# The last keys of V by halves of the heads in a fused decode kernel

## The chip, the cores and the metric

The kernel runs on one core of a Trainium2 chip. The metric is the device time of one execution in microseconds; the time before is the median of three runs.

## The reference

Two branches work on the same eight tokens and are mixed by a gate:

```python
q = (x @ wq).reshape(B, Sq, H, Dh).transpose(0, 2, 1, 3)         # B 8, Sq 1, D 576, H 32, Dh 128
scores = einsum("bhqd,bhkd->bhqk", q, k_cache) * (Dh ** -0.5)    # Sk 4096 keys
o = einsum("bhqk,bhkd->bhqd", softmax(scores), v_cache)
a = o.transpose(0, 2, 1, 3).reshape(B, Sq, H * Dh) @ wo
b = gelu(layernorm(x) @ w1 + b1) @ w2 + b2                       # hidden 4608
g = sigmoid((x * gate_w).sum(-1))
return g * a + (1 - g) * b
```

All tensors are bf16. The K and V caches, 268 MB each, are nearly all the bytes.

## The kernel before

The attention is cut into 32 groups. A group is one token and eight heads (`HB`). Its K (or V) is 8 MB and lies on 128 partitions: sixteen partitions (`RH`) for each head, 256 keys on each partition. Partitions 0 to 63 so hold heads 0 to 3 of the group, and 64 to 127 heads 4 to 7.

For each group VectorE multiplies K with the query in eight chunks (`mult`, line 465), TensorE sums the products (lines 476 and 179), VectorE reduces them (line 484) and runs the softmax, and TensorE multiplies the probabilities with V (`pv`, line 527). In `pv` the probabilities are the stationary operand, and a tile `P` holds them spread over the eight heads with zeros where partition and head don't match (`own`). ScalarE evicts the sums (`evict`), TensorE gathers them by head (`gather`, line 545), and VectorE normalises.

Instructions are recorded in order for each engine by `op`, and semaphore waits are worked out from the records that an operation names. All bulk loads are issued by SyncE, in the order in which they are recorded; a load waits until its buffer is free. `load` gives a transfer a semaphore of its own.

The last group (`last`) is handled apart. Its V arrives in eight pieces (`V_LAST`, keys per partition), into the buffer `VL`, a view of K's. The first 192 keys of each partition go through `pv`. For the rest, from `T_TURN` on, the roles are turned (`pv_turned`, line 653): V is the stationary operand, one matmul for each key of a partition, and the sums for eight heads appear as columns 0 to 7 of the PSUM bank `qb_ps`; `gather` adds the first 192 keys there. `norm_turned` (line 662) multiplies by the reciprocal sums `rz` and writes into `OT_sb`, and `a_proj` runs the last eight heads through the output projection, four matmuls for each head (`quarters`, line 590). The projections of the other 24 heads are done before. Last, line 735 combines both branches, and four stores write the output.

The bias `b2` is broadcast from memory into rows of `b2_4`, in four groups that begin at partitions 0, 32, 64 and 96, of which eight rows each are used in the output. `load_b2` issues its transfers on ScalarE's queue, at the fourth group before the last; `b_gate` on GpSimd adds it.

Of the kernel before, what the change touches and what calls it, by code (L numbers as in the profile page):

```python
# [6 lines left out]
ACT = mybir.ActivationFunctionType  # L7
ALU = mybir.AluOpType
AX = mybir.AxisListType
BF16 = mybir.dt.bfloat16  # L10
F32 = mybir.dt.float32
# [11 lines left out]
HB = 8  # L23
RH = 128 // HB
NHG = H // HB
NG = NHG * B
NTT = SK // RH
# [7 lines left out]
TQ = 4  # L35
QN = D // 4
# [5 lines left out]
class Stream:  # L42
# [10 lines left out]
    def op(self, engine, fn, waits=(), dma=None, side=0):  # L53

        rec = [fn, [w for w in waits if w is not None], None, dma, (engine, side)]
        self.ops[engine].append(rec)
        if dma is not None:
            return ("dma", *dma)
        return ("op", engine, rec)
# [81 lines left out]
def bass_gated_mix__mha_block_cached__mixer_channel_mlp__decode_kernel(  # L141
# [18 lines left out]
    op = S.op  # L160
# [4 lines left out]
    def pstride(t):  # L165
        return t[tuple([slice(None)] * len(t.shape))].ap[0][0]

    def view(t, offset, shape):
        ap = []
        stride = 1  # L170
        for n in reversed(shape[1:]):
            ap.insert(0, [stride, n])
            stride *= n
        return bass.AP(tensor=t, offset=offset, ap=[[pstride(t), shape[0]]] + ap)
# [23 lines left out]
    VL = view(KR, 0, [128, NTT, DH])  # L198
    p1 = sb("p1", [128, 2, CT, DH], BF16)

    P_last = view(p1, 0, [128, NTQ, HB, TQ])
# [19 lines left out]
    b2_4 = sb("b2_4", [128, QN], BF16)  # L221
# [5 lines left out]
    q_bc = sb("q_bc", [128, B, NHG * DH], BF16)  # L227
    OT_sb = sb("OT_sb", [128, H, B], BF16)
    bmg_sb = view(up_f, 0, [128, QN])
    out_sb = sb("out_sb", [128, QN], BF16)  # L230
    g4 = sb("g4", [128, 2], F32)
    ident = sb("ident", [128, 128], BF16)
# [6 lines left out]
    shift = sb("shift", [128, SW + 128], BF16)  # L239
# [4 lines left out]
    mB = sb("mB", [128, 32], F32)  # L244
# [10 lines left out]
    rz = sb("rz", [128, HB], F32)  # L255
# [4 lines left out]
    o_ps = bank[2:4]  # L260
    qb_ps = bank[4]
    oz_ps = bank[5]
    up_ps = bank[6]
# [7 lines left out]
    def load(engine, dst, src, name, waits=()):  # L271
        return op(engine, lambda e: e.dma_start(dst, src), waits, dma=(nc.alloc_semaphore(name), 16))  # L272
# [8 lines left out]
    c_b2 = op("gpsimd", lambda e: e.memset(b2_4[:], 0.0))  # L281
# [12 lines left out]
    def kv_src(cache, n):  # L294
        hg, b = divmod(n, B)
        return cache[b, hg * HB:(hg + 1) * HB].rearrange("h (p t) d -> (h p) t d", p=RH)

    k_done, v_done = {}, {}
    k_land, v_land = {}, {}
# [24 lines left out]
        t = op("sync", lambda e: e.dma_start(dst, src), [*waits, v_done.get(n - 1)], dma=(sV, 16 * nV[0]))  # L324
        v_land[n] = [(t, VB, 0, 0, NTT)]

    def load_v_part(n, buf, at, t0, t1, waits):

        src = kv_src(A_v_cache, n)[:, t0:t1, :]
        dst = buf[:, at:at + t1 - t0, :]  # L330
        t = load("sync", dst, src, f"sVp{n}_{t0}", waits)
        v_land.setdefault(n, []).append((t, buf, at - t0, t0, t1))

    V_LAST = (128, 32, 32, 16, 16, 16, 8, 8)
    T_TURN = NTK + 64

    last = NG - 1
    load_k_half(0, 0)
# [17 lines left out]
    def blank(ps):  # L356
# [5 lines left out]
        out=own[:, :], in_=ident[:, :].rearrange("p (h r) -> p h r", h=HB), axis=AX.X, op=ALU.add), [c_id])  # L362
    c_fine = aside("vector", lambda e: e.tensor_reduce(
        out=fine[:, :], in_=bass.AP(tensor=ident, offset=0, ap=[[pstride(ident), 128], [1, RD], [RD, RH]]),
        axis=AX.X, op=ALU.max), [c_id])
    c_shift = aside("vector", lambda e: e.tensor_reduce(
        out=shift[:, SW:SW + RH], in_=ident[:, :].rearrange("p (a r) -> p a r", r=RD), axis=AX.X, op=ALU.max),
        [c_id, c_shift])
    c_Sel = aside("scalar", lambda e: e.activation(
        out=Sel[:].rearrange("p b (h r) -> p b h r", h=4),  # L370
        in_=bass.AP(tensor=ident, offset=0, ap=[[pstride(ident), 128], [1, B], [32, 4], [0, RH]]), func=ACT.Copy), [c_id])


    t = op("vector", lambda e: e.tensor_reduce(out=stat[:, 0:1], in_=x_sb, axis=AX.X, op=ALU.add), [ld_x])
    t1 = op("vector", lambda e: e.tensor_tensor_reduce(out=junk, in0=x_sb, in1=x_sb, scale=1.0, scalar=0.0,
                                                       op0=ALU.mult, op1=ALU.add, accum_out=stat[:, 1:2]))
    t = op("vector", lambda e: e.tensor_scalar(out=stat[:, 2:3], in0=stat[:, 0:1], scalar1=1.0 / D, scalar2=None,
                                               op0=ALU.mult), [t])
    t = op("vector", lambda e: e.tensor_tensor(out=stat[:, 3:4], in0=stat[:, 2:3], in1=stat[:, 2:3], op=ALU.mult), [t])
    t = op("vector", lambda e: e.scalar_tensor_tensor(out=stat[:, 6:7], in0=stat[:, 1:2], scalar=1.0 / D,  # L380
                                                      in1=stat[:, 3:4], op0=ALU.mult, op1=ALU.subtract), [t, t1])
# [30 lines left out]
    t = op("vector", lambda e: e.reciprocal(out=stat[:, 7:8], in_=stat[:, 5:6]), [a_sqrt])  # L412
# [8 lines left out]
    for half in range(2):  # L421
        for h in range(4):
            for kt in range(NKT):
                o = tr_ps[half][32 * h:32 * h + B, :]
                at = (kt * SK + half * (SK // 2) if kt < NKF else NKF * SK) + h * DH
                r = bass.AP(tensor=VB, offset=at, ap=[[pstride(VB), 128], [4 * DH, 4], [1, DH]])
                xi = kt if kt < NKF else NKF + half
                p_Q = aside("tensor", lambda e, o=o, r=r, kt=kt, xi=xi: e.matmul(
                    o, lhsT=xT_sb[:, xi, :], rhs=r, start=(kt == 0), stop=(kt == NKT - 1)),
                    [v_xT, *ld_wq, *c_ps] if h == kt == half == 0 else ())  # L430
        a_Q.append(aside("scalar", lambda e, half=half: e.activation(
            out=Q4[:, half * 512:(half + 1) * 512], in_=tr_ps[half][:, :], func=ACT.Copy, scale=inv_sqrt_dh), [p_Q]))
# [5 lines left out]
    a_qb, v_mult, v_red, p_sum, v_nm, a_exp, v_P, p_pv, a_ev, p_oz, v_norm, v_rs, p_z, v_rz = ({} for _ in range(14))  # L438
# [9 lines left out]
    a_q, a_O = {}, {}  # L448
# [71 lines left out]
    def pv(n, parts):  # L520
        for i in parts:
            land, buf, shift, t0, t1 = v_land[n][i]
            for tq in range(t0 // TQ, t1 // TQ):
# [5 lines left out]
                    rhs=buf[:, at:at + TQ, :].rearrange("p t d -> p (t d)"),  # L529
                    start=(tq < 4), stop=(tq >= (NTQ if n < last else T_TURN // TQ) - 4)), w)  # L530
        v_done[n] = p_pv[n]
# [6 lines left out]
    def evict(n):  # L538
        a_ev[n] = op("scalar", lambda e: e.activation(out=O_sb[:].rearrange("p t d -> p (t d)"), in_=o_ps[n // last][:, :],  # L539
                                                      func=ACT.Copy), [p_pv[n], p_oz.get(n - 1)])  # L540
# [15 lines left out]
    st = {}  # L556
# [30 lines left out]
    def quarters(lhsT, w, first, stop, waits, end=aside):  # L587

        for i in range(4):
            last = (end if i == 3 else aside)("tensor", lambda e, i=i: e.matmul(  # L590
                y_ps[32 * i:32 * i + B, 0:QN], lhsT=lhsT, rhs=w[:, i * QN:(i + 1) * QN], start=first, stop=stop),
                waits if i == 0 else ())
        return last

    def load_b2():
        st["ld_b2"] = [
            load("scalar", b2_4[32 * i + r:32 * i + r + m, :],
                 bass.AP(tensor=B_b2.tensor, offset=B_b2.offset + i * QN, ap=[[0, m], [1, QN]]), f"ld_b2{i}_{r}", [c_b2])
            for i in range(4) for r, m in ((0, 5), (5, 3))]

    def down_proj(j0, j1):
        for jt in range(j0, j1):
# [36 lines left out]
            out=o.rearrange("p r b -> p (r b)"), in_=up_ps[:, 0:RD * B], func=ACT.Copy), [st["p_rows"]])  # L639
        st["rows", hg] = st["a_rows"]  # L640

    def a_proj(hg):
        for h in range(hg * HB, (hg + 1) * HB):
            st["p_a"] = quarters(OT_sb[:, h, :], wo_sb[:, h, :], h == 0, h == H - 1,
                                 [st.get(("rows", hg)), a_O.get(min(hg * B + B - 1, NG - 2)), v_norm.get(NG - 1),
                                  st["ld_wo" if hg < NHG - 1 else "ld_wo3"], st["a_bx"]] if h == hg * HB else ())


    def pv_turned(n, parts):
        for i in parts:  # L650
            land, buf, shift, t0, t1 = v_land[n][i]
            for t in range(t0, t1):
                p_oz[n] = op("tensor", lambda e, t=t, buf=buf, at=t + shift: e.matmul(  # L653
                    qb_ps[:, 0:HB], lhsT=buf[:, at, :], rhs=P_last[:, t // TQ, :, t % TQ], start=(t == T_TURN), stop=(t == NTT - 1)),
                    [land, v_P[n]] if t == t0 else ())

    def recip(n):
        v_rz[n] = op("vector", lambda e: e.reciprocal(out=rz[:, :], in_=oz_ps[:, HB:2 * HB]), [p_z[n]])

    def norm_turned(n):  # L660
        hg, b = divmod(n, B)
        v_norm[n] = op("vector", lambda e: e.tensor_tensor(  # L662
            out=OT_sb[:, hg * HB:(hg + 1) * HB, b], in0=qb_ps[:, 0:HB], in1=rz[:, :], op=ALU.mult),
            [p_oz[n], v_rz[n]])


    q_of(0)
# [2 lines left out]
    for n in range(NG):  # L670
# [14 lines left out]
        if n == 0:  # L685
# [5 lines left out]
                out=selO[:].rearrange("p t h -> p h t"),  # L691
                in_=bass.AP(tensor=ident, offset=0, ap=[[pstride(ident), 128], [TQ, HB], [1, TQ], [32, 4]]),
# [3 lines left out]
            for i in range(4):  # L696
                a_g4 = aside("scalar", lambda e, i=i: e.activation(out=g4[32 * i:32 * i + B, :], in_=stat[:, G_COL:G_COL + 2],
                                                                func=ACT.Copy), [v_omg, c_g4])
# [19 lines left out]
        if n == last - 4:  # L718
            load_b2()
            b_gate()  # L720
    t0 = 0
    for nt in V_LAST:
        load_v_part(last, VL, t0, t0, t0 + nt, [k_done[last, 0]])
        t0 += nt
    pv(last, (0,))
    total(last)
    recip(last)
    pv(last, (1, 2))
    evict(last)
    pv_turned(last, (3,))  # L730
    gather(last)
    pv_turned(last, range(4, len(V_LAST)))
    norm_turned(last)
    a_proj(NHG - 1)
    t = op("vector", lambda e: e.scalar_tensor_tensor(  # L735
        out=out_sb[0:QP, :], in0=y_ps[0:QP, 0:QN], scalar=g4[0:QP, 0:1], in1=bmg_sb[0:QP, :],
        op0=ALU.mult, op1=ALU.add), [st["p_a"], st["g_bmg"], a_g4])
# [45 lines left out]
```

## Time and profile before

| | |
|---|---|
| median of 3 runs | 1298.17 us (1297.94 to 1298.27) |
| profiled execution | 1298.21 us |
| its span, first to last instruction | 1296.3 us |
| mean granted TensorE clock | 0.834 |
| bytes moved, mean rate over the span | 557.12 MB, 430 GB/s |

The profile is of one execution. PE is TensorE's matmuls, PEld its weight loads, DVE is VectorE, ACT ScalarE, POOL GpSimd, SP SyncE. Times in the trace count from the first instruction of the span; the execution's own time is some 2 us longer than the span. A row of a view names the line of the kernel, the engine, the operation, and `out<-in` by the program's names.

### The profile page before, as it was taken

Reading aid. Unit: us, or ns where it says so; the run is one execution under the profiler, and the core shown is the slowest. Engines: PE = TensorE matmul, PEld = TensorE weight load, DVE = VectorE, ACT = ScalarE, POOL = GpSimd, SP = SyncE. Lnnn points to the kernel's source line nnn. Section 1 sums busy time; section 2 is a strip of 40 time slices with the busy share of each in tenths; the row PEclk is TensorE's granted clock in tenths of the full one; section 3 lists DMA queues with packets and bytes.
Section 4 is the critical chain, followed back from the end, with each engine's and each line's share of the span. In section 5 each row is a group of like instructions: output and inputs, shape, how many; then the busy total and the mean of one; then the engine's idle time right before and its main releaser. Section 6 shows DMA issues by size and latency. Waiting matters only on the chain.

```text
span 1296.3 us, 10765 instructions
## 1 busy us (share of the span) xinstructions
PE 739.2 (57%) x5044; PEld 152.9 (12%) x3252; DVE 851.1 (66%) x1075; ACT 68.8 (5%) x163; POOL 10.4 (1%) x23
## 2 busy tenths in 40 slices
PE   3955556555556555556555556645556655546646
PEld 0521111011111001111001111001111001111003
DVE  3646667766668766667766667766667776667771
ACT  3100000000000000000000000000000000000000
POOL 0010000000000000000000000000000000000000
PEclk8877898778888877888887799878789877888886
DMA  9999999999999999999999999999999999999997
GB/s 405 430 440 429 441 425 433 441 427 441 427 431 441 427 441 429 431 441 427 439 431 431 441 425 439 433 431 441 425 437 435 429 443 425 437 433 431 441 417 327
DMA packets 12987, 557.12 MB, mean 430 GB/s; under 512 B 1568, under 2 KB 2608, under 8 KB 3504
## 3 DMA queue, kind: packets, MB, share of 16 engines
q1 hardware_dynamic: 12704, 556.93, 99.5%
q8 instruction: 7, 0.11, 0.0%
q10 hardware_dynamic: 272, 0.04, 0.0%
q14 instruction: 4, 0.03, 0.0%
HBM read 556.96 MB, written 0.01 MB: 430 GB/s over the span
## 4 chain that ended last, share of the span: by engine, by line
DMA 68%; DVE 19%; PE 9%; issue 3%; SPq 0%; DVEq 0%
DMA KR<-in_A_k_cache_dram 67%; DVE p L465 16%; PE psb L179 7%; DVE s_sb L484 2%; DMA KR<-in_A_v_cache_dram 2%; PE psb L476 2%; SPq L272 0%; DVEq L134 0%; PE psb L590 0%; PE psb L653 0%; DVE out_sb L735 0%; DVE OT_sb L662 0%
## 5 line engine op out<-in xcount | busy, mean ns | idle before, releaser
L465 DVE TENSOR_TENSOR p<-KR,q_n 128x4096 bf16<-128x4096 bf16 x256 | 582.0, 2284 | 229.7 <-DMA KR<-in_A_k_cache_dram 229.7
L179 PE MATMUL psb<-p,ident 128*128 128x512 bf16 x1792 | 482.9, 415 | 0.0
L476 PE MATMUL psb<-p,ident 128*128 128x512 bf16 x256 | 111.4, 435 | 504.5 <-DVE p L465 504.5
L484 DVE TENSOR_REDUCE s_sb<-psb 128x32 f32<-128x512 f32 x256 | 175.2, 684 | 90.8 <-PE psb L179 90.8
L476 PEld LDWEIGHTS psb<-p,ident 128*128 128x128 bf16 x256 | 26.1, 102 | 950.9 <-DVE p L465 950.4
L527 PE MATMUL psb<-VB,P 128*32 128x512 bf16 x1984 | 115.0, 385 | 4.5 <-DMA VB<-in_A_v_cache_dram 4.5
L513 DVE TENSOR_SCALAR P<-E,own 128x256 bf16<-128x256 bf16 x248 | 51.7, 284 | 84.3 <-ACT E L510 84.3
L527 PEld LDWEIGHTS psb<-VB,P 128*32 128x32 bf16 x1984 | 50.6, 98 | 54.4 <-DMA VB<-in_A_v_cache_dram 4.7
L452 ACT ACTIVATE q_n<-q_bc 128x128 bf16<-128x128 bf16 x32 | 9.9, 309 | 865.9 <-DVE p L465 865.9
L545 PE MATMUL psb<-selO,O_sb 128*128 128x8 f32 x256 | 33.9, 259 | 21.8 <-ACT O_sb L539 21.8
L545 PEld LDWEIGHTS psb<-selO,O_sb 128*128 128x128 f32 x256 | 31.0, 191 | 37.1 <-ACT O_sb L539 37.1
L539 ACT ACTIVATE O_sb<-psb 128x512 f32<-128x512 f32 x32 | 19.1, 597 | 176.6 <-PE psb L527 176.6
L566 PE MATMUL psb<-yT_sb,KR 128*128 128x8 bf16 (+1 forms) x216 | 19.6, 229 | 0.0
L566 PEld LDWEIGHTS psb<-yT_sb,KR 128*128 128x128 bf16 (+1 forms) x216 | 18.4, 165 | 2.7 <-issue 1.4
L534 PEld LDWEIGHTS psb<-rs,ones 128*128 128x128 f32 x64 | 12.3, 194 | 46.0 <-issue 45.2
L510 ACT ACTIVATE E<-s_sb,mD 128x256 bf16<-128x256 f32 x32 | 16.0, 499 | 9.7 <-DVE mD L509 9.6
L501 DVE TENSOR_REDUCE mA<-s_sb 128x1 f32<-128x256 f32 x32 | 13.4, 420 | 1.1
L516 DVE TENSOR_REDUCE es<-E 128x1 f32<-128x256 bf16 x32 | 13.2, 412 | 0.0
L550 DVE RECIPROCAL rz<-psb 128x8 f32<-128x8 f32 x31 | 6.2, 201 | 9.0 <-PE psb L545 9.0
L457 ACT ACTIVATE OT_sb<-O_n 128x8 bf16<-128x8 bf16 x31 | 7.4, 237 | 84.5 <-DVE O_n L551 84.5
L534 PE MATMUL psb<-rs,ones 128*128 128x8 f32 x64 | 9.4, 219 | 0.0
L517 DVE TENSOR_SCALAR rs<-own,es 128x8 f32<-128x8 f32 x32 | 8.5, 265 | 1.1
(81 smaller groups left out, 109.7 us busy)
## 6 DMA issues: line engine op xcount, KB each, us to landing
KR<-in_A_k_cache_dram SPq DMA_DIRECT2D x2, 4096.0 KB, 27.2
VB<-in_A_v_cache_dram SPq DMA_DIRECT2D x1, 5376.0 KB, 21.0
VB<-in_B_w_dram SPq DMA_DIRECT2D x1, 5184.0 KB, 39.5
KR<-in_B_w_dram SPq DMA_DIRECT2D x1, 4608.0 KB, 43.3
VB<-in_A_wq_dram SPq DMA_DIRECT2D x1, 4096.0 KB, 12.6
KR<-in_A_v_cache_dram SPq DMA_DIRECT2D x1, 4096.0 KB, 17.9
KR<-in_A_wo_dram SPq DMA_DIRECT2D x1, 3456.0 KB, 24.7
VB<-in_A_v_cache_dram SPq DMA_DIRECT2D x1, 2816.0 KB, 38.7
```

The lines of the kernel that those rows point to most:

```text
L179: return e.add_instruction(mybir.InstMatmult(name=nc.get_next_instruction_name(), engine=mybir.EngineType.PE, ins=[e.lower_ap(rhs), e.lowe ...
L465: v_mult[n, c] = op("vector", lambda e: e.tensor_tensor(out=p1[:, par, :, :], in0=k, in1=qb, op=ALU.mult), [k_land[n, s], a_q[n], p_sum.ge ...
L476: fn = lambda e, r=r: e.matmul(tr_ps[par][:, :], lhsT=ident[:, :], rhs=r, start=True, stop=False)
L484: v_red[n, c] = op("vector", lambda e: e.tensor_reduce(out=s_sb[:, at:at + CT], in_=tr_ps[par][:, :].rearrange("p (t c) -> p t c", c=CH), ...
L501: t = op("vector", lambda e: e.tensor_reduce(out=mA[:, 0:1], in_=s_sb[:, :], axis=AX.X, op=ALU.max), [v_red[n, NC - 1], c_mA])
L510: a_exp[n] = op("scalar", lambda e: e.activation(out=E[:, :], in_=s_sb[:, :], func=ACT.Exp, bias=mD[:, 0:1], scale=1.0), [v_nm[n], v_P.get ...
L513: v_P[n] = op("vector", lambda e, h=h: e.tensor_scalar(out=(P if n < NG - 1 else P_last)[:, :, h, :], in0=E[:, :].rearrange("p (q t) -> p ...
L527: p_pv[n] = op("tensor", lambda e, o=o, tq=tq, at=at, buf=buf: e.matmul(o, lhsT=(P if n < last else P_last)[:, tq, :, :].rearrange("p h t ...
L534: p_z[n] = op("tensor", lambda e: e.matmul(oz_ps[:, HB:2 * HB], lhsT=ones[:, :], rhs=rs[:, :], start=True, stop=True), [v_rs[n], v_norm.ge ...
L539: a_ev[n] = op("scalar", lambda e: e.activation(out=O_sb[:].rearrange("p t d -> p (t d)"), in_=o_ps[n // last][:, :], func=ACT.Copy), [p_p ...
L545: p_oz[n] = op("tensor", lambda e, tt=tt: e.matmul(o, lhsT=O_sb[:, tt, :], rhs=selO[:, tt, :], start=(tt == 0 and n < last), stop=(tt == T ...
L566: st["p_up"] = (op if end else aside)("tensor", lambda e, w=w, o=o, kt=kt: e.matmul(o, lhsT=w, rhs=yT_sb[:, kt, :], start=(kt == 0), stop= ...
```

## The change

The last 32 keys per partition no longer come in pieces over all 128 partitions. They come first for heads 0 to 3 (partitions 0 to 63) in two pieces of 16 keys, then for heads 4 to 7 (partitions 64 to 127) in pieces of 16, 8 and 8. Keys 192 to 223 are left as they were.

The sums of the first half gather in the bank `up_ps`, those of the second in `o_ps[0]`. What `qb_ps` holds by then, keys 0 to 223 of all heads, is copied by VectorE (`take`). For the first half VectorE adds that copy to its sums and multiplies by `rz`. For the second half TensorE adds the copy into the bank ahead of the V matmuls, by a matmul with an f32 unit matrix (`give`); the matrix is made by ScalarE (`unit`) in the space of `q_bc`. The output projection of heads 0 to 3 waits for the first norm alone, that of heads 4 to 7 for the second. On TensorE both stand behind the last V matmul. The first half's V matmuls use 64 rows of weights, the second half's all 128 (the probabilities of partitions 0 to 63 are zero there), both with four columns.

`load_b2` issues one transfer per group instead of two (of 5 and 3 rows), of 16, 13, 10 and 8 rows.

```diff
+    unit_sb = view(q_bc.bitcast(F32), 0, [128, 128])
...
-    def load_v_part(n, buf, at, t0, t1, waits):
-
-        src = kv_src(A_v_cache, n)[:, t0:t1, :]
-        dst = buf[:, at:at + t1 - t0, :]
+    def load_v_part(n, buf, at, t0, t1, waits, h0=0, h1=HB):
+
+        src = kv_src(A_v_cache, n)[h0 * RH:h1 * RH, t0:t1, :]
+        dst = buf[h0 * RH:h1 * RH, at:at + t1 - t0, :]
...
-    V_LAST = (128, 32, 32, 16, 16, 16, 8, 8)
+    V_LAST = ((128, 0, HB), (32, 0, HB), (32, 0, HB), (16, 0, HB), (16, 0, HB),
+              (16, 0, HH), (16, 0, HH), (16, HH, HB), (8, HH, HB), (8, HH, HB))
     T_TURN = NTK + 64
+    T_HALF = NTT - 32
...
-            load("scalar", b2_4[32 * i + r:32 * i + r + m, :],
-                 bass.AP(tensor=B_b2.tensor, offset=B_b2.offset + i * QN, ap=[[0, m], [1, QN]]), f"ld_b2{i}_{r}", [c_b2])
-            for i in range(4) for r, m in ((0, 5), (5, 3))]
+            load("scalar", b2_4[32 * i:32 * i + m, :],
+                 bass.AP(tensor=B_b2.tensor, offset=B_b2.offset + i * QN, ap=[[0, m], [1, QN]]), f"ld_b2{i}", [c_b2])
+            for i, m in enumerate((16, 13, 10, 8))]
...
+            o = {(0, HB): qb_ps, (0, HH): up_ps, (HH, HB): o_ps[0]}[h0, h1]
             for t in range(t0, t1):
-                p_oz[n] = op("tensor", lambda e, t=t, buf=buf, at=t + shift: e.matmul(
-                    qb_ps[:, 0:HB], lhsT=buf[:, at, :], rhs=P_last[:, t // TQ, :, t % TQ], start=(t == T_TURN), stop=(t == NTT - 1)),
+                p_oz[n] = op("tensor", lambda e, t=t, buf=buf, at=t + shift, h0=h0, h1=h1, o=o: e.matmul(
+                    o[:, h0:h1], lhsT=buf[0:h1 * RH, at, :], rhs=P_last[0:h1 * RH, t // TQ, h0:h1, t % TQ],
+                    start=(t == (T_HALF if h0 < h1 < HB else T_TURN)), stop=t in (T_HALF - 1, NTT - 1)),
...
+    def unit():
+        t = op("scalar", lambda e: e.activation(out=unit_sb, in_=ident[:, :], func=ACT.Copy), [a_q[last]])
+        st["a_unit"] = t
+
+    def take(n):
+
+        st["v_take"] = op("vector", lambda e: e.tensor_copy(out=mB[:, 0:HB], in_=qb_ps[:, 0:HB]), [p_oz[n]])
+
+    def give(n):
+        op("tensor", lambda e: e.matmul(o_ps[0][:, HH:HB], lhsT=unit_sb, rhs=mB[:, HH:HB], start=True, stop=False),
+           [st["v_take"], st["a_unit"]])
...
     evict(last)
+    unit()
     pv_turned(last, (3,))
     gather(last)
-    pv_turned(last, range(4, len(V_LAST)))
-    norm_turned(last)
-    a_proj(NHG - 1)
+    pv_turned(last, (4,))
+    take(last)
+    pv_turned(last, (5, 6))
+    norm_turned(last, 0, HH)
+    t = v_norm[last]
+    give(last)
+    pv_turned(last, (7, 8, 9))
+    norm_turned(last, HH, HB)
+    v_norm[last], t = t, v_norm[last]
+    a_proj(NHG - 1, 0, HH)
+    v_norm[last] = t
+    a_proj(NHG - 1, HH, HB)
```

More of the change, by code (lines that the diff above doesn't have):

```diff
@@ L325, in load_v @@
         v_land[n] = [(t, VB, 0, 0, NTT)]
-    def load_v_part(n, buf, at, t0, t1, waits):
-        src = kv_src(A_v_cache, n)[:, t0:t1, :]
-        dst = buf[:, at:at + t1 - t0, :]
-        t = load("sync", dst, src, f"sVp{n}_{t0}", waits)
+    def load_v_part(n, buf, at, t0, t1, waits, h0=0, h1=HB):
+        src = kv_src(A_v_cache, n)[h0 * RH:h1 * RH, t0:t1, :]
+        dst = buf[h0 * RH:h1 * RH, at:at + t1 - t0, :]
+        t = load("sync", dst, src, f"sVp{n}_{t0}_{h0}", waits)
         v_land.setdefault(n, []).append((t, buf, at - t0, t0, t1))
-    V_LAST = (128, 32, 32, 16, 16, 16, 8, 8)
+        v_heads[n, len(v_land[n]) - 1] = (h0, h1)
+    v_heads = {}
+    HH = HB // 2
+    V_LAST = ((128, 0, HB), (32, 0, HB), (32, 0, HB), (16, 0, HB), (16, 0, HB),
+              (16, 0, HH), (16, 0, HH), (16, HH, HB), (8, HH, HB), (8, HH, HB))
     T_TURN = NTK + 64
+    T_HALF = NTT - 32
     last = NG - 1
@@ L640, in to_rows, with a_proj @@
         st["rows", hg] = st["a_rows"]
-    def a_proj(hg):
-        for h in range(hg * HB, (hg + 1) * HB):
+    def a_proj(hg, h0=0, h1=HB):
+        for h in range(hg * HB + h0, hg * HB + h1):
             st["p_a"] = quarters(OT_sb[:, h, :], wo_sb[:, h, :], h == 0, h == H - 1,
                                  [st.get(("rows", hg)), a_O.get(min(hg * B + B - 1, NG - 2)), v_norm.get(NG - 1),
-                                  st["ld_wo" if hg < NHG - 1 else "ld_wo3"], st["a_bx"]] if h == hg * HB else ())
+                                  st["ld_wo" if hg < NHG - 1 else "ld_wo3"], st["a_bx"]] if h == hg * HB + h0 else ())
     def pv_turned(n, parts):
@@ L651, in pv_turned @@
             land, buf, shift, t0, t1 = v_land[n][i]
+            h0, h1 = v_heads[n, i]
+            o = {(0, HB): qb_ps, (0, HH): up_ps, (HH, HB): o_ps[0]}[h0, h1]
             for t in range(t0, t1):
-                p_oz[n] = op("tensor", lambda e, t=t, buf=buf, at=t + shift: e.matmul(
-                    qb_ps[:, 0:HB], lhsT=buf[:, at, :], rhs=P_last[:, t // TQ, :, t % TQ], start=(t == T_TURN), stop=(t == NTT - 1)),
+                p_oz[n] = op("tensor", lambda e, t=t, buf=buf, at=t + shift, h0=h0, h1=h1, o=o: e.matmul(
+                    o[:, h0:h1], lhsT=buf[0:h1 * RH, at, :], rhs=P_last[0:h1 * RH, t // TQ, h0:h1, t % TQ],
+                    start=(t == (T_HALF if h0 < h1 < HB else T_TURN)), stop=t in (T_HALF - 1, NTT - 1)),
                     [land, v_P[n]] if t == t0 else ())
@@ L658, in recip, with norm_turned @@
         v_rz[n] = op("vector", lambda e: e.reciprocal(out=rz[:, :], in_=oz_ps[:, HB:2 * HB]), [p_z[n]])
-    def norm_turned(n):
-        hg, b = divmod(n, B)
-        v_norm[n] = op("vector", lambda e: e.tensor_tensor(
-            out=OT_sb[:, hg * HB:(hg + 1) * HB, b], in0=qb_ps[:, 0:HB], in1=rz[:, :], op=ALU.mult),
-            [p_oz[n], v_rz[n]])
+    def unit():
[6 more added lines that the diff above has]
+           [st["v_take"], st["a_unit"]])
+    def norm_turned(n, h0, h1):
+        hg, b = divmod(n, B)
+        o = OT_sb[:, hg * HB + h0:hg * HB + h1, b]
+        if h1 < HB:
+            t = op("vector", lambda e: e.tensor_tensor(
+                out=mB[:, HB:HB + HH], in0=up_ps[:, h0:h1], in1=mB[:, 0:HH], op=ALU.add), [p_oz[n], st["v_take"]])
+            v_norm[n] = op("vector", lambda e: e.tensor_tensor(
+                out=o, in0=mB[:, HB:HB + HH], in1=rz[:, h0:h1], op=ALU.mult), [t, v_rz[n]])
+        else:
+            v_norm[n] = op("vector", lambda e: e.tensor_tensor(
+                out=o, in0=o_ps[0][:, h0:h1], in1=rz[:, h0:h1], op=ALU.mult), [p_oz[n], v_rz[n]])
     q_of(0)
@@ L720, in bass_gated_mix__mha_block_cached__mixer_channel_mlp__decode_kernel @@
             b_gate()
[L721 to L724, printed above, removed]
+    t0 = dict.fromkeys(range(HB), 0)
+    for nt, h0, h1 in V_LAST:
+        load_v_part(last, VL, t0[h0], t0[h0], t0[h0] + nt, [k_done[last, 0]], h0, h1)
+        t0.update({h: t0[h] + nt for h in range(h0, h1)})
     pv(last, (0,))
```

## The prediction

> **What bounds the kernel now.** I read the page first (the busy shares, the queues, the chain), then the last pieces of the chain in order of time, then TensorE's timeline and a table of narrow windows over the same last microseconds.
>
> ```profile
> span 1296.3 us, 10765 instructions
> PE 739.2 (57%) x5044; PEld 152.9 (12%) x3252; DVE 851.1 (66%) x1075; ACT 68.8 (5%) x163; POOL 10.4 (1%) x23
> DMA packets 12987, 557.12 MB, mean 430 GB/s; under 512 B 1568, under 2 KB 2608, under 8 KB 3504
> q1 hardware_dynamic: 12704, 556.93, 99.5%
> q10 hardware_dynamic: 272, 0.04, 0.0%
> DMA 68%; DVE 19%; PE 9%; issue 3%; SPq 0%; DVEq 0%
> ```
>
> No compute engine is over 66%, while the packets of SyncE's queue q1 fill 99.5% of the time of the 16 DMA engines. The kernel is a stream of 557 MB at 430 GB/s with a short tail of compute behind it. The change moves no byte less of K or V, so it can act in two places only: how the last megabyte is streamed, and what follows the last landing. The chain shows the second:
>
> ```profile
> 1267.23 24.38 DMA KR<-in_A_v_cache_dram
> 1291.61 0.05 issue
> 1291.66 0.39 PE psb L653 x8
> 1292.05 0.02 issue
> 1292.07 0.20 DVE OT_sb L662
> 1292.28 0.04 issue
> 1292.32 1.16 PE psb L590 x32
> 1293.48 0.03 issue
> 1293.51 0.37 DVE out_sb L735
> ```
>
> The last piece of V lands at 1291.61 (the columns are start and length). Eight matmuls, one normalisation, 32 projection matmuls and one combination follow, each waiting for the one before. The stores run from there to the span's end; the change doesn't touch them.
>
> ```profile
> 1287.88 0.56 PE L653 MATMUL psb<-p,KR 128*128 128x8 bf16 x16 [0.59 <-DMA KR<-in_A_v_cache_dram]
> 1288.30 1.04 PE L545 MATMUL psb<-selO,O_sb 128*128 128x8 f32 x8
> 1289.19 0.54 PE L653 MATMUL psb<-p,KR 128*128 128x8 bf16 x16
> 1290.40 0.99 PE L653 MATMUL psb<-p,KR 128*128 128x8 bf16 x24 [0.67 <-DMA KR<-in_A_v_cache_dram]
> 1291.66 0.38 PE L653 MATMUL psb<-p,KR 128*128 128x8 bf16 x8 [0.26 <-DMA KR<-in_A_v_cache_dram]
> 1292.32 1.13 PE L590 MATMUL psb<-KR,OT_sb 128*8 128x144 bf16 x32 [0.29 <-DVE OT_sb L662]
> ```
>
> In this view of TensorE alone (start, length, instruction, and in brackets the idle time before it) the engine waits for landings up to the last one; its own work at the end is small. How the DMA engines run dry is in the windows. The last two columns are the busy share of the 16 engines and GB/s:
>
> ```profile
> 1287.00:1288.00 1.00, 0.41 (x13) 0.12 (x6) 0.00 (x0) 0.60 (x1) 0.00 (x0) 1.00 1.03 412
> 1288.50:1289.00 0.50, 0.50 (x7) 0.50 (x6) 0.00 (x0) 0.00 (x0) 0.00 (x0) 1.00 0.89 344
> 1289.00:1289.50 0.50, 0.50 (x16) 0.50 (x17) 0.00 (x0) 0.00 (x0) 0.00 (x0) 1.00 0.70 270
> 1289.50:1290.00 0.50, 0.23 (x10) 0.14 (x6) 0.00 (x0) 0.00 (x0) 0.00 (x0) 1.00 0.55 213
> 1290.00:1290.50 0.50, 0.10 (x4) 0.10 (x4) 0.00 (x0) 0.00 (x0) 0.00 (x0) 0.69 0.37 139
> 1290.50:1291.00 0.50, 0.49 (x16) 0.40 (x15) 0.00 (x0) 0.00 (x0) 0.00 (x0) 0.50 0.10 37
> 1291.00:1291.30 0.30, 0.28 (x8) 0.28 (x8) 0.00 (x0) 0.00 (x0) 0.00 (x0) 0.50 0.02 7
> ```
>
> The engines don't end together. They drop out one by one from 1288.5 to about 1291.2, 2.7 us. The busy time left after 1288.5 is 0.5 x (0.89 + 0.70 + 0.55 + 0.37 + 0.10) = 1.3 us for the mean engine, so the mean one ends at 1289.8, and the last one 1.4 us later sets the end. Roughly half are still at work at 1290.0. The landing at 1291.61 follows the last bytes by about 0.4 us.
>
> **The tail of compute: a gain.** Before, the 32 projection matmuls start 0.27 us after the last V matmul (1292.05 to 1292.32): two hand-overs and the 0.20 us normalisation. After the change the first 16 of them, for heads 0 to 3, need only the first norm. They stand ahead of the second half's 16 on TensorE and take about half of 1.16, 0.58 us. The second norm costs 0.26 with its hand-overs and runs beside them. So 0.27 us goes, and what is late next is TensorE itself: 8 + 32 matmuls back to back after the last landing, whose sum doesn't change. I take 0.25; with full cover and overlapped starts it could be 0.35.
>
> What is added on TensorE must be done before the last landing. V takes 32 + 32 matmuls for the 32 keys instead of 32, so 32 more; 16 cost 0.54 us by the row at 1289.19, so 1.1 us more. `give` is one f32 matmul, which counts as two instructions; eight such take 1.04 us at L545, so 0.26. Together 1.4 us, between 1289.7 and the last landing, where TensorE before has 0.67 + 0.26 us of waits and 24 matmuls. If the landings stayed where they are, the second piece of the first half would come where the piece of 16 came (the start at 1290.40), its 16 matmuls would be through at 1290.95, `give` at 1291.2, and 32 matmuls of the second half, two times 0.54 less the overlap of the two groups, at 1292.15 to 1292.3, against 1292.05 before. So 0.1 to 0.25 us of the gain would be lost. If the landings come later, TensorE waits and the 0.25 stands whole.
>
> The other added work is off the path. These rows price it (mean ns behind the bar; for line 272 shortest, median and longest ns, and the first and last start):
>
> ```profile
> L452 ACT ACTIVATE q_n<-q_bc 128x128 bf16<-128x128 bf16 x32 | 9.9, 309 | 865.9 <-DVE p L465 865.9
> L551 DVE TENSOR_TENSOR O_n<-psb,rz 128x8 bf16<-128x8 f32 x31 | 5.1, 166 | 1.1
> 1287.35 0.60 ACT L539 ACTIVATE O_sb<-psb 128x512 f32<-128x512 f32 x1 [7.05 <-PE psb L527]
> L272 ACTq DMA_DIRECT2D b<-in_B_b_dram x8: 262/293/294, 1118.4 to 1120.7; - x8
> L272 SPq DMA_DIRECT2D KR<-in_A_v_cache_dram x8: 328/430/433, 1263.7 to 1267.2; - x8
> KR<-in_A_v_cache_dram SPq DMA_DIRECT2D x1, 4096.0 KB, 17.9
> ```
>
> `unit` is one ScalarE copy of 128x128 (309 ns) behind the eviction that ends at 1287.95, done by 1288.3; ScalarE has nothing after it but stores. `take` on VectorE waits for the matmuls that end at 1289.73 and costs some 0.2 us. Queued behind it are only the first half's addition and product, which wait for a later landing anyway, and TensorE's `give`, which comes later still. That addition and product, two of some 0.2 us, end half a microsecond after the first half's matmuls, under the second half's landings. SyncE issues ten V transfers for eight: two more of 0.43 us plus a gap move the last issue from 1267.2 to 1268.2. The first of them alone is 4 MB, about 10 us of streaming, so no engine runs dry; without that cover it would cost 0.9 us.
>
> **b2.** ScalarE issues four transfers instead of eight, saving 1.2 us at 1118 on an engine that is 5% busy: nothing. Rows written go from 8 x 4 = 32 to 16 + 13 + 10 + 8 = 47; only the first 8 of each group reach the output. The packets of q10 took under 0.05% of 16 engines over 1296 us, under 10.4 us for 272, so under 38 ns each. Fifteen more rows with at most a completion each are 30 packets, under 1.2 engine-us, or 0.07 us per engine. They don't fall evenly, though. One engine may get some 8 packets more or fewer, 0.3 us either way, and in a stream without idle time that stays with the engine up to the end. I take zero, and plus or minus 0.3 for the range.
>
> **The last megabyte: the disputed cost.** The bytes are the same. Before, the 32 keys come as pieces of 16, 8 and 8 over 128 partitions; now as 16, 16 over partitions 0 to 63 and 16, 8, 8 over 64 to 127. No row shows a transfer into half of the partitions. The lower end: each engine's 1/16 of the megabyte takes 65.5 KB / (430/16 GB/s) = 2.44 us whatever its target, cost 0 (a gain is excluded but for hundredths, since the engine's bytes stay). The upper end: a write into half of the partitions runs at half of the kernel's rate, 215 GB/s, and the two halves come strictly one after the other: 4.88 us, cost 2.44. Which value? Suppose two engines share one way into a half. Only engines that are in the same half at the same time hinder each other. With a lag d between the two, up to 1.22 us, the later one loses 1.22 - d in each half, 2.44 - 2d in all. The drain gives the lags. About half of the engines end within 1290.0 to 1291.2, and two of those lie some 0.4 apart on average (a third of 1.2), so a pair of late ones loses about 1.6 us; a late one with an early one loses little. Among eight pairs one of two late engines is nearly sure. It would have ended at 1290.4 to 1291.2 and now ends at 1292.0 to 1292.8, against 1291.2: +0.8 to +1.6, and some more if two lie closer. I take +1.5, nearer to the upper end of this than its middle, since the worst of several pairs counts.
>
> [...]
>
> **The sum.** 0 (issues, unit, take, b2) + 1.5 - 0.25 = +1.25 us. The profiled execution took 1298.21 with a span of 1296.3, and the median is 1298.17, 0.04 below: 1299.4.
>
> **Rivals.** (1) Half-width writes cost nothing. For: the packets are no smaller in bytes per partition (4096 and 2048 as before), and the rate of the mean engine, 430/16 GB/s, may be its own limit. Against: the stream that shows 430 GB/s always writes all 128 partitions, so it shows no spare capacity in half of them. TensorE then gives back 0.1 to 0.25 of its 0.25: 1298.17 - 0.15 to 1298.17, so 1298.1. (2) The halves are strictly one after another. Place: the stretch from about 1287 to the last landing; price: 2.44 us at exactly half the rate, with 0.25 given back: 1300.4. The point from which it decides for slower is a half-width rate of 200 GB/s: 1.05 MB / 200 = 5.24, so +2.80 - 0.25 = +2.55, 0.2% of the time. For it: each half is a transfer of its own, in order. Against: the drain shows the engines 2.7 us apart, more than the 1.2 us of a half, so they are not in one half together. (3) The halves travel side by side, each served by its own eight engines. Each of those carries twice the rows, at no loss, but the first half lands with the last piece. Then up to 16 + 32 matmuls and `give` stand behind it, 0.54 + 0.26 + 1.0, where 0.39 stood: +1.4 - 0.25, 1299.3. Against: nothing in the queue rows says that a transfer is served by some engines only.
>
> **Numbers.** Shared halves, my forecast, 0.50: 1299.4, own range 1298.7 to 1300.0. Rival 1: 0.25. Rival 2: 0.15, of it 0.08 past 200 GB/s. Rival 3: 0.05. The rest, 0.05, is a shift of the engines' order by b2 beyond what I bounded, 0.02 of it for better and 0.03 for worse. The range 1297.7 to 1300.9 takes in rivals 1 and 2 with b2's 0.3. About 0.2% (2.6 us) is what a measurement of this kernel can tell from no change, so all but the far end of rival 2 lies within: faster 0.02 (a gain of 2.6 us would need more than the 1.4 us by which the last engine trails the mean and the 0.27 together), same 0.87, slower 0.08 + 0.03 = 0.11.
>
> **What would show it.** In the changed profile: V matmuls into two more PSUM banks; 32 projection matmuls right behind the last 8 of V without the 0.29 us wait on VectorE (step one right); the last landing at about 1293.1 and windows after 1287 with a DMA share near 1 at clearly under 400 GB/s (sharing right), or the old drain with a landing at 1291.6 (rival 1). A landing past 1294 at about 215 GB/s is rival 2. The forecast is wrong if the first half's matmuls wait next to the last landing, or if the drain before 1287 is already shifted, which would be b2's doing.

## The result and the profile after

| | before | changed |
|---|---|---|
| median of 16 runs | 1298.19 us | 1300.49 us (1299.94 to 1301.80) |
| ratio to before | | 1.0019, 95% interval 1.0011 to 1.0027 |
| profiled execution, its span | 1298.21, 1296.3 us | 1300.48, 1298.5 us |

The change costs 2.3 us, where the prediction had 1.25. The page's first lines say that the body of the stream is as before: DMA fills 99.5% of the time again.

```profile
span 1298.5 us, 10834 instructions
DMA packets 12986, 557.14 MB, mean 429 GB/s; under 512 B 1630, under 2 KB 2670, under 8 KB 3502
q1 hardware_dynamic: 12672, 556.93, 99.5%
q10 hardware_dynamic: 302, 0.05, 0.0%
```

The end of the chain, in order of time (start, length, what), differs:

```profile
1267.61 25.03 DMA KR<-in_A_v_cache_dram
1292.64 0.05 issue
1292.69 0.59 PE psb L661 x16
1293.28 0.52 PE psb L678 x2
1293.79 0.85 PE psb L661 x32
1294.65 1.09 PE psb L596 x24
1295.73 0.03 issue
1295.76 0.37 DVE out_sb L772
```

The landing that decides is no longer the last one. It is that of the first half's second piece, at 1292.64. From there TensorE runs without a gap: 16 matmuls, `give` (0.52), 32 matmuls of the second half, the projection. The very last piece lands while the second half's matmuls run; the issue on SyncE and the time to its landing show when:

```profile
1269.52 0.60 SPq L273 DMA_DIRECT2D KR<-in_A_v_cache_dram  x1
```

```profile
DMA to landing us min/median/max: 24.4/24.4/24.4
```

That is 1293.9, against 1291.6 before. So the transfers end 2.3 us later, and the combination starts 1.85 us behind the last landing (1295.76) where it took 1.90 (1291.61 to 1293.51). The windows over the end show why the transfers are late (the last two columns are DMA share and GB/s):

```profile
1287.00:1288.00 1.00, 0.81 (x8) 0.00 (x0) 0.00 (x0) 0.13 (x1) 0.00 (x0) 0.50 1.08 221
1288.50:1289.00 0.50, 0.00 (x0) 0.00 (x0) 0.00 (x0) 0.17 (x1) 0.00 (x0) 0.50 1.11 246
1289.50:1290.00 0.50, 0.50 (x14) 0.50 (x11) 0.00 (x0) 0.00 (x0) 0.00 (x0) 0.50 1.06 225
1290.50:1291.00 0.50, 0.50 (x4) 0.50 (x4) 0.00 (x0) 0.00 (x0) 0.00 (x0) 0.50 0.77 156
1291.50:1292.00 0.50, 0.50 (x17) 0.48 (x16) 0.00 (x0) 0.00 (x0) 0.00 (x0) 0.50 0.52 152
1292.50:1293.00 0.50, 0.43 (x16) 0.34 (x14) 0.00 (x0) 0.00 (x0) 0.00 (x0) 0.50 0.20 61
```

From 1287 to 1288 the engines are as busy as before (1.08 against 1.03) and move 221 GB/s instead of 412. They don't lack work; the packets take longer for their bytes.

### The profile page after: what moved, and what is told of

Its sections match the earlier page's. It is cut to its first block, busy times and chain, and to the rows that moved or that the text cites. A ratio compares the mean times of both kernels' runs of the same rounds, so it can differ in the third digit from the quotient of the medians.

```text
span 1298.5 us, 10834 instructions
## 1 busy us (share of the span) xinstructions
PE 742.8 (57%) x5078; PEld 155.0 (12%) x3286; DVE 851.9 (66%) x1078; ACT 69.0 (5%) x164; POOL 11.8 (1%) x23
## 3 DMA queue, kind: packets, MB, share of 16 engines
q1 hardware_dynamic: 12672, 556.93, 99.5%
## 4 chain that ended last, share of the span: by engine, by line
DMA 68%; DVE 18%; PE 9%; issue 3%; SPq 0%; DVEq 0%
DMA KR<-in_A_k_cache_dram 66%; DVE p L471 16%; PE psb L179 8%; DVE s_sb L490 2%; DMA KR<-in_A_v_cache_dram 2%; PE psb L482 2%; SPq L273 0%; DVEq L134 0%; PE psb L661 0%; PE psb L596 0%; PE psb L678 0%; DVE out_sb L772 0%
```

## Experiments

Times below stand beside runs of the kernel before on the same chip, whose median was 1298.03 to 1298.14 us.

**b2 alone.** The kernel before with the new rows:

```diff
-            for i in range(4) for r, m in ((0, 5), (5, 3))]
+            for i, m in enumerate((16, 13, 10, 8))]
```

> The kernel before with only b2's rows changed (16, 13, 10 and 8 in four transfers). Theory A (transfers into 64 neighbouring partitions share half of the ways into SBUF and run at half the rate): b2 does nothing, 1298.2 us within 0.3, last landing at 1291.6 within 0.3. Theory B (b2's uneven rows push the slowest DMA engine back): most of the 2.3 us, 1299.5 or more, with the last landings late already in the pieces ahead of the last 32 keys.

Measured 1298.12 us, ratio 1.0001 (0.9992 to 1.0010), with the last landing at 1291.25 in its profile (span 1295.9 us, 1296.3 before), a little earlier than A's 1291.3 to 1291.9. b2 does nothing that can be measured. In the changed kernel's page q10 has 302 packets for 272: thirty more, as counted.

**The changed kernel with b2 as before.**

```diff
-            for i, m in enumerate((16, 13, 10, 8))]
+            for i in range(4) for r, m in ((0, 5), (5, 3))]
```

> The changed kernel with b2 loaded as before. Theory A: as the changed kernel, 1300.2 to 1300.7 us, last landing near 1293.9. Theory B (b2): back to about 1298.2 us.

Measured 1300.32 us, ratio 1.0019 (1.0010 to 1.0028), with the last landing at 1294.1. All of the loss is in the halves. TensorE's timeline shows at which piece it begins:

```profile
1288.72 0.56 PE L661 MATMUL psb<-p,KR 128*128 128x8 bf16 x16 [1.55 <-DMA KR<-in_A_v_cache_dram]
1289.14 1.04 PE L551 MATMUL psb<-selO,O_sb 128*128 128x8 f32 x8
1291.30 1.77 PE L661 MATMUL psb<-p,KR 128*128 128x8 bf16 x48 [1.13 <-DMA KR<-in_A_v_cache_dram]
```

The first and third row begin with the two pieces of 16 keys that still go to all 128 partitions. Before, TensorE began them at 1287.88 and 1289.19; here it waits for them until 1288.72 and 1291.30. So two microseconds are lost on pieces ahead of the halves.

**The transfers alone.** Transfers and order as in the changed kernel, computation as before:

```diff
...
+    for nt, t0, p in ((16, 224, slice(0, 64)), (16, 240, slice(0, 64)), (16, 224, slice(64, 128)),
+                      (8, 240, slice(64, 128)), (8, 248, slice(64, 128))):
+        tail.append((nt, t0, p, load("sync", VL[p, t0:t0 + nt, :], ...)))
+    for t0, t1, i in ((224, 240, (0, 2)), (240, 248, (1, 3)), (248, 256, (1, 4))):
+        v_land[last].append(([tail[j][3] for j in i], VL, 0, t0, t1))
```

> The kernel before with the last 32 keys fetched in the changed kernel's five transfers by halves and in their order, all computation as before (each group of keys waits for both of its halves), b2 as before. Theory A: the last landing moves to about 1293.9 and the old tail of 1.9 us stands behind it: 1300.3 to 1300.7 us, even though TensorE has nothing more to do. Theory C (TensorE's 32 more matmuls and the added f32 matmul set the end): 1298.2 us, as TensorE's work is the old one.

Measured 1301.04 us, ratio 1.0024 (1.0014 to 1.0034): 3.0 us, with TensorE's work unchanged. That is more than the whole change and above A's range, and far from C's 1298.2. The transfers cost 3.0; beside the changed kernel with b2 as before, on the same chip, the computation by halves gives 0.7 of it back, though the two intervals overlap.

**The computation alone.** By halves as changed, over transfers as before:

```diff
-              (16, 0, HH), (16, 0, HH), (16, HH, HB), (8, HH, HB), (8, HH, HB))
+              (16, 0, HB), (8, 0, HB), (8, 0, HB))
...
-    pv_turned(last, (5, 6))
+    pv_turned(last, (5,), (0, HH))
+    give(last)
+    pv_turned(last, (5,), (HH, HB))
+    pv_turned(last, (6,), (0, HH))
+    pv_turned(last, (6,), (HH, HB))
+    pv_turned(last, (7,), (0, HH))
     norm_turned(last, 0, HH)
     t = v_norm[last]
-    give(last)
-    pv_turned(last, (7, 8, 9))
+    pv_turned(last, (7,), (HH, HB))
```

> The changed kernel's computation by halves (two sums, take, give, two norms, projection in two parts) over transfers as before (16, 8 and 8 keys over all 128 partitions, each used first for heads 0 to 3, then for heads 4 to 7), b2 as before. Theory A: the transfers are the old ones, last landing 1291.6; behind it 16 matmuls instead of 8 (0.2 us more) and no wait for a norm (0.27 us less): 1298.0 to 1298.3 us. Theory C (TensorE): 1299 us or more.

Measured 1299.01 us, ratio 1.0007 (0.9998 to 1.0016): 1.0 us above the kernel before, in theory C's range and not in A's, though the interval reaches the kernel before. The chain:

```profile
1290.12 0.04 issue
1290.17 0.55 PE psb L661 x16
1290.72 0.52 PE psb L678 x2
1291.23 1.35 PE psb L661 x40
1292.58 0.02 issue
1292.61 0.17 DVE mB L685
1292.78 0.02 issue
1292.80 0.19 DVE OT_sb L687
```

With landings where they were, TensorE sets the end from 1290.17 on. 58 instructions fill the 2.4 us up to 1292.58; 40 of them take 1.35, 34 ns each. The hand-over to VectorE is there again, since only eight matmuls are left to cover the first norm's two operations.

**The same without `unit` and `give`**, the second half added on VectorE as the first is:

```diff
-    unit()
...
-    give(last)
...
+        src = up_ps if h1 < HB else o_ps[0]
+        t = op("vector", lambda e: e.tensor_tensor(
+            out=mB[:, HB + h0:HB + h1], in0=src[:, h0:h1], in1=mB[:, h0:h1], op=ALU.add), ...)
...
```

> As the kernel with the computation by halves over transfers of all 128 partitions, which came to 1299.0 us, but without unit and give: the second half's sums get keys 0 to 223 added on VectorE as the first half's do. Theory F (TensorE's queue near the end sets the time there; the f32 unit matmul took 0.52 us of it): 1298.3 to 1298.7 us. Rival G (the 0.9 us comes from the chain of norms on VectorE): 1299.0 us or more, since VectorE gets one more operation of 0.17 us.

Measured 1298.65 us, ratio 1.0004 (0.9995 to 1.0013), inside F's range. That is 0.5 us above the kernel before on its chip, where the run with `give` was 1.0 above on another; the two intervals overlap. In its profile the gather's eight instructions took 1.88 us, about as in the changed kernel's (1.85 at a granted clock of 0.50) and not as before (1.04 at 1.00), so the single trace doesn't price `give` cleanly. No version of the computation by halves was faster than the kernel before.

**The 128-key piece in two halves.** The same cost on a piece of 4 MB:

```diff
+        for p in parts:
+            src = kv_src(A_v_cache, n)[p, t0:t1, :]
+            dst = buf[p, at:at + t1 - t0, :]
+            ts.append(load("sync", dst, src, ...))
...
+                    (slice(0, 64), slice(64, 128)) if t0 == 0 else (slice(0, 128),))
```

> The kernel before with its 128-key piece (4 MB) fetched as two transfers, partitions 0 to 63 and 64 to 127; all else as before. Theory A (half the ways, half the rate): 262 KB per engine take up to 9.75 us more; less twice the lag between engines, at most some 2.7 us: 6 to 9.8 us slower, 1304 to 1308 us, with about 220 GB/s over some 15 us. Theory D (each more transfer, or a transfer's small size, costs a fixed part of the 2.3 us seen for two more of them): 1298.2 to 1299.5 us.

Measured 1311.79 us, ratio 1.0104 (1.0087 to 1.0120): 13.7 us, well above A's range. One long window, and TensorE's row for the V of the group before (group 30), first in this run, then in the kernel before:

```profile
1269.00:1293.00 24.00, 6.05 (x72) 2.92 (x72) 2.06 (x10) 0.84 (x2) 0.00 (x0) 0.70 0.92 191
```

```profile
1275.61 4.99 PE L529 MATMUL psb<-VB,P 128*32 128x512 bf16 x64 [8.10 <-DMA VB<-in_A_v_cache_dram]
```

```profile
1271.92 5.89 PE L527 MATMUL psb<-VB,P 128*32 128x512 bf16 x64 [4.52 <-DMA VB<-in_A_v_cache_dram]
```

191 GB/s is under half of 430. And the V of group 30, a transfer to all partitions issued over 30 us earlier (at 1230.6 in the profile before, where the pieces of the last V follow from 1263.75), is late: TensorE began on it at 1271.92 before and begins at 1275.61 here. That engines still at the old transfer are held up by those already in the first half is the author's reading and not shown; the profile shows the delay, not the single engines.

**Even and odd partitions** instead of two blocks:

```diff
-                    (slice(0, 64), slice(64, 128)) if t0 == 0 else (slice(0, 128),))
+                    (slice(0, 128, 2), slice(1, 128, 2)) if t0 == 0 else (slice(0, 128),))
```

> As the kernel with the 128-key piece in two transfers of 64 partitions, but the first takes the even partitions and the second the odd ones. Theory A (it matters which partitions: 0 to 63 reach half of the ways, every second one of 0 to 127 all of them): within 1 us of before, 1298 to 1299.2 us. Theory E (64 partitions are slow whichever they are): as slow as the split at partition 64, 1304 to 1308 us.

Measured 1298.08 us, ratio 1.0000 (0.9990 to 1.0010). 64 partitions, the same bytes, the same number of transfers, and nothing is lost:

```profile
1271.66 5.12 PE L529 MATMUL psb<-VB,P 128*32 128x512 bf16 x64 [4.08 <-DMA VB<-in_A_v_cache_dram]
```

```profile
1269.00:1281.00 12.00, 6.18 (x72) 2.98 (x72) 2.14 (x11) 0.83 (x2) 0.00 (x0) 0.86 0.93 397
```

**Four quarters** of 32 neighbouring partitions:

```diff
+                    (slice(0, 32), slice(32, 64), slice(64, 96), slice(96, 128)) if t0 == 0 else ...
```

> The 128-key piece in four transfers of 32 neighbouring partitions (0 to 31, 32 to 63, 64 to 95, 96 to 127). [...] Theory E (the rate goes with the number of partitions): a quarter of the rate, 20 us slower or more, 1318 us and up.

Measured 1310.55 us, ratio 1.0096 (1.0079 to 1.0113), not distinguishable from two halves. A quarter of the partitions isn't slower than a half (198 GB/s from 1269 to 1294, where the halves had 191 from 1269 to 1293), so it isn't their number. Why blocks of neighbouring partitions are slow isn't shown: the runs give times and rates for each choice of partitions, not the ways into them that theory A speaks of.

**The even and odd partitions at the change's own place**, five transfers of the same sizes:

```diff
-    for nt, t0, p in ((16, 224, slice(0, 64)), (16, 240, slice(0, 64)), (16, 224, slice(64, 128)),
+    for nt, t0, p in ((16, 224, slice(0, 128, 2)), (16, 240, slice(0, 128, 2)), (16, 224, slice(1, 128, 2)),
...
```

> As the kernel with the five transfers alone (computation as before, b2 as before), but the two halves are the even and the odd partitions. Sizes, number and order of the transfers are those of the changed kernel. Theory A (ways into SBUF, by which partitions lie together): the whole cost goes, 1298.0 to 1298.4 us, last landing 1291.3 to 1291.8. Theory D (five small transfers instead of three): stays near 1301 us.

Measured 1298.29 us, ratio 1.0002 (0.9993 to 1.0011). The 3.0 us are gone. q1's row is that of the changed kernel (12672 packets, 556.93 MB). So neither the size nor the number of the transfers costs anything here; the choice of partitions does.

```profile
1287.00:1288.00 1.00, 0.53 (x21) 0.47 (x17) 0.00 (x0) 0.60 (x1) 0.00 (x0) 1.00 1.04 416
```

**Alternating halves**, first on another chip than the kernel with the transfers alone, then both again on one chip:

```diff
-    for nt, t0, p in ((16, 224, slice(0, 64)), (16, 240, slice(0, 64)), (16, 224, slice(64, 128)),
+    for nt, t0, p in ((16, 224, slice(0, 64)), (16, 224, slice(64, 128)), (16, 240, slice(0, 64)),
...
-    for t0, t1, i in ((224, 240, (0, 2)), (240, 248, (1, 3)), (248, 256, (1, 4))):
+    for t0, t1, i in ((224, 240, (0, 1)), (240, 248, (2, 3)), (248, 256, (2, 4))):
```

> As the kernel with the five transfers alone (1301.0 us), but first and second half alternate: 16 keys of partitions 0 to 63, 16 of 64 to 127, 16, then 8 and 8. Theory H (late engines are held up while they still write their last pieces for all 128 partitions, because early ones crowd the ways of the first half): the crowding is spread over both halves, some 0.7 to 1.5 us are won, 1299.5 to 1300.3 us. Rival I (the loss comes from engines that are in the same half together, as the prediction had it): no gain, 1300.7 to 1301.3 us.

> The five transfers by halves alone, again, on one chip with the alternating order, because the two had run on different chips. 1300.4 to 1301.1 us under every theory; it is the base for the other.

> The alternating order beside the plain one on the same chip. Theory H (alternating spreads the crowding): 0.4 us or more below the plain order. Rival I (the order of the halves doesn't matter, the 0.5 us between the two was the chips): within 0.3 us of it.

Measured 1300.51 us for the alternating order (1.0018, 1.0009 to 1.0027), then on the common chip 1300.94 for the plain order (1.0024, 1.0015 to 1.0033) and 1300.33 for the alternating one (1.0017, 1.0008 to 1.0026). The gain of 0.5 to 0.6 us was found both times, as H's second text asks and I's doesn't, but the intervals overlap, and both times lie just above H's first range. Nor does it come as H has it. In the first pair of profiles TensorE begins the last piece for all partitions at the same time in both, the plain order first, then the alternating one:

```profile
1290.81 0.59 PE L655 MATMUL psb<-p,KR 128*128 128x8 bf16 x16 [1.03 <-DMA KR<-in_A_v_cache_dram]
```

```profile
1290.85 0.59 PE L655 MATMUL psb<-p,KR 128*128 128x8 bf16 x16 [0.20 <-DMA KR<-in_A_v_cache_dram]
```

In the second pair that piece begins at 1290.56 in the plain order and at 1291.17 in the alternating one. So the delay ahead of the halves was not relieved; what was won lies within them. From issue and time to landing, the last piece lands 3.4 us behind the last piece for all partitions in both plain profiles (1290.7 to 1294.1, 1290.5 to 1293.9), and 2.5 in both alternating ones (1290.8 to 1293.3, 1291.1 to 1293.6), where it was 2.4 before (1289.2 to 1291.6). How the loss divides among engines stays open.

## Why the prediction was right or wrong

Range, sign and verdict held: 1300.49 lies within 1297.7 to 1300.9 and within 0.2%. But the size was short by 1.1 us. The time is above the forecast's own range (1298.7 to 1300.0), and nearer to the strict rival (1300.4) than to 1299.4. The wide range held because it took the strict rival in. And 0.2% was too coarse for what a measurement can tell: the interval, from 1.0011 on, leaves out 1.

- **b2, issues, unit, take: 0.** Right. b2 alone gave 1.0001. The issues took longer than costed: the last one started at 1269.5, not 1268.2, because a transfer by halves takes 0.6 us of SyncE instead of 0.43, and because the first one of this execution started 0.6 later (1264.34 for 1263.75). It stayed hidden behind the 4 MB piece: with even and odd partitions there are ten issues as well, and nothing is lost (1298.29 us, 1298.14 before).
- **The last megabyte: +1.5.** That transfers by halves cost time was right, the term too small: the last landing moved by 2.3 us in the changed kernel's profile, and the transfers alone cost 3.0 and 2.85 us in two comparisons. The step that failed is the sentence that only engines in the same half at the same time hinder each other, so that lags between engines spare time. That two engines share a way into a half was the author's supposition; no run shows it, and which engines meet was not traced. What the runs show is that with transfers by halves in the queue, transfers to all partitions ahead of them are late too: group 30's V reached TensorE 3.7 us later with the 4 MB piece in halves, and in the changed kernel the piece of keys 208 to 223, from its issue and its time to landing, lands at 1291.5, against 1289.2 before.

```profile
L273 SPq DMA_DIRECT2D KR<-in_A_v_cache_dram x1: 433/433/433, 1266.2 to 1266.2; - x1
...
DMA to landing us min/median/max: 25.3/25.3/25.3
```

```profile
L272 SPq DMA_DIRECT2D KR<-in_A_v_cache_dram x1: 433/433/433, 1265.6 to 1265.6; - x1
...
DMA to landing us min/median/max: 23.6/23.6/23.6
```

  That is 2.3 us lost by the landing of the last piece ahead of the halves, as much as the whole delay of the last landing in this profile. In the two profiles of the transfers alone it is 1.5 of 2.5 us and 1.3 of 2.3; there some 1.0 us more is lost within the halves, where the prediction had all of its 1.5. By the same working the delay begins shortly before: in the changed kernel keys 160 to 191 land on time (1286.7 for 1286.6), keys 192 to 207 1.3 us late (1289.2 for 1287.9).
- **The upper end of 2.44 for it**, half the rate throughout, was no bound either: on the 4 MB piece, where it would have been 9.75, 13.7 were lost.
- **The tail of compute: -0.25.** The wait for the norm did go (no gap between lines 661 and 596). The gain in the profiled execution is 0.05, because TensorE was not free at the last landing: its queue set the end from 1292.64 on, with 16 matmuls in 0.59 us, `give` in 0.52, where 0.26 was costed, and 32 matmuls in 0.85. The prediction named this loss, but only for landings that stay, and said that later landings would hide it. They didn't, because the first half's landings were late as well. In the kernel with b2 as before the same chain starts and ends 0.2 earlier:

```profile
1292.44 0.05 issue
...
1295.56 0.37 DVE out_sb L772
```

  Both take 3.1 us from the landing of the first half's second piece to the combination. The last landing, at 1294.1 there, is 0.2 later than in the changed kernel's profile, so that by it the gain is 0.4: the time behind the last landing no longer measures the tail. Against the transfers alone the computation by halves was worth 0.7 us over the runs of one chip. The gather isn't on this chain. It took 1.04 us there, and 1.85 in the changed kernel's profile, where the granted clock was 0.50:

```profile
1289.67 1.85 PE L551 MATMUL psb<-selO,O_sb 128*128 128x8 f32 x8
```

- **The rivals.** Half-width writes for nothing: excluded for blocks of neighbouring partitions (3.0 us lost at the change's own place, 13.7 on the 4 MB piece), true for even and odd ones (1298.29 against 1298.14, and 1298.08 against 1298.08). What it gave for the computation by halves when the landings stay, 1298.1, was too low for the order that was run: 1299.01, and 1298.65 without `give`. Strictly one after another: its signs, a landing past 1294 at about 215 GB/s, nearly came (1293.9; 221 GB/s from 1287 to 1288). The picture isn't right: the DMA share falls from 1.06 at 1289.5 to 0.20 at 1292.5, so the engines were not in step, and 1.3 us or more of the loss lie ahead of the halves. Side by side: not seen, as the first half's second piece landed 1.3 us ahead of the last.

## What to carry to other kernels

With transfers into blocks of neighbouring partitions the stream ran here at under half its rate (191 GB/s over 24 us, 430 over the span before), and a transfer to all partitions issued earlier was late (V of group 30, by 3.7 us); with transfers into every second partition of 128 it did not (397 GB/s from 1269 to 1281, 395 before) and that V was on time (1271.66, 1271.92 before). When the work after the last landing is to be shortened, look first at what the new transfers do to the stream, since 0.27 us of waiting was bought here with landings 2.3 to 2.5 us later. An f32 matmul that must fit between landings should be costed at the clock granted at the end, not at that of the row it is taken from: `give` took 0.52 us at a granted clock of 0.50, where the gather's row at 1.00 gave 0.26. For the bf16 matmuls the difference was small (16 in 0.59 us at 0.50, in 0.54 at 1.00).

## What was not expected of the hardware

- Below half: 191 GB/s over 24 us with halves of 2 MB, 430 GB/s over the span before.
- A transfer that was issued more than 30 us earlier was late: V of group 30 reached TensorE 3.7 us later with the 4 MB piece in halves.
- TensorE's clock: the gather (four f32 matmuls, eight instructions) took 1.85 us in the changed kernel's profile and 1.04 us before. The granted clock in those windows was 0.50 and 1.00.
